# Keeping VectorE's unused allowance for one more unit, and computing the gates later, in a four-layer attention kernel

## Chip, cores and metric

The kernel runs on one core of a Trainium2 chip. A core has five engines that run side by side, each taking its own instructions strictly in order: TensorE (PE, matrix multiplication; PEld are its weight loads), VectorE (DVE), ScalarE (ACT, activation functions), GpSimd (POOL) and SyncE (SP, which issues the transfers here). Engines wait for each other through semaphores. The metric is the device time of one execution in microseconds (us); lower is better. The time before is 2142.66 us, the median of three runs (2138.74 to 2143.29).

## What is computed

Four layers over 2,048 tokens of width 512, with 32 heads of 16. Layers 0 and 2 (kind A) work in four segments of 512 tokens: causal attention inside a segment, mixed by a gate per head with a memory that earlier segments have filled. Layers 1 and 3 (kind B) are full attention over all tokens.

```python
def _A_ref(x, wq, wk, wv, wo, beta):           # N = 4 segments, per head
    ...
    g = _sigmoid(beta).reshape(1, H, 1, 1)
    for s in range(N):
        logits = jnp.einsum('bhqd,bhkd->bhqk', qs, ks) * scale + mask
        p = _softmax(logits, axis=-1)
        a_dot = jnp.einsum('bhqk,bhkd->bhqd', p, vs)
        pq = phi(qs)
        num = jnp.einsum('bhld,bhde->bhle', pq, M)
        den = jnp.einsum('bhld,bhd->bhl', pq, z)[..., None] + 1e-06
        outs.append(g * (num / den) + (1.0 - g) * a_dot)
        pk = phi(ks)
        M = M + jnp.einsum('bhld,bhle->bhde', pk, vs)
        z = z + jnp.einsum('bhld->bhd', pk)
    ...
def _B_ref(x, wqkv, wo):
    ...
    scores = jnp.einsum('bhqd,bhkd->bhqk', q, k) * Dh ** (-0.5)
    p = _softmax(scores, axis=-1)
    o = jnp.einsum('bhqk,bhkd->bhqd', p, v)
    ...
x = x + _A_ref(_layernorm(x), ...); x = x + _B_ref(_layernorm(x), ...)
x = x + _A_ref(_layernorm(x), ...); x = x + _B_ref(_layernorm(x), ...)
```

## The kernel before

The program is written out at build time by a planner (class `Builder`), which decides the order of every engine's instructions; the chip then follows that order.

**Units.** The attention work is cut into *units*. A unit takes up to three *banks*; a bank is 128 keys by 512 queries of scores for one head, made by TensorE from masked queries `qm` and keys (`KA`, `KB`). `unit` issues the score matmuls into one of two sets of three PSUM banks, and then one exponential by ScalarE over all three (line 1039, `pT<-ps`). Banks of kind A are also masked by GpSimd (line 1054). Two units later (three for kind A) `pv_step` multiplies the exponentials by the values (`VA`, `VB`), adding up in PSUM bank 6. Eight heads of a chunk and query segment are two *groups* of up to 64 banks each; when a group has all its products, `finish` has VectorE transpose the accumulator out of bank 6 (line 1099, `tT`), takes reciprocals of the softmax sums (line 1103), and GpSimd scales (line 1112). The next group accumulates into the same bank 6.

**VectorE's share of the exponentials.** `dx_pick` may take one more bank out of a group per unit and give its exponential to VectorE instead of ScalarE. Its scores go to PSUM bank 7; VectorE reads them out (`dx_first`, line 748), and once two such banks are there a chain of six instructions computes the exponential by a polynomial (`dx_chain`, lines 772 to 782, tiles `dxo`, `dxz`). `dx_pick` refuses while the VectorE allowance is below -300 ns, while a buffer or a spacing rule forbids it, or when little attention work is left in stock (`low`, under 24 banks).

**Background work.** Everything else (layer norms, projections, the memory, output projections, and the steps of `dx_chain`) is cut into steps held by generator tasks. A step says what it needs, how many halves of a PSUM bank's matmuls it costs on TensorE, and its nominal time on VectorE. Projections and outputs use PSUM bank 7 too. In each turn of the main loop `attention` issues one unit, then `credit` grants an allowance: 2 (kind A) or 3 (kind B) on TensorE and 1,300 or 1,420 ns on VectorE, or 5 and 2,600 when the stock is low. `background` then runs steps while both allowances are positive and VectorE's, with 300 ns of slack, covers the step. `finish` and the transposes of finished chunks (`run_deferred`) are charged to the same allowance. What a unit leaves unused does not carry over: `credit` caps the allowance at one unit's grant. An overdraft does carry over.

```python
858  def credit(self, pe, dve):
860      self.cr_pe = min(self.cr_pe + pe, pe)
861      self.cr_dve = min(self.cr_dve + dve, dve)
```

**Fillers.** `keep_busy` adds multiplications by a tile of zeros (`ps<-wB,zero`) so that TensorE has 1,024 columns of extra work in each unit.

**The gates.** `gates` computes sigmoid(beta) (`gtok`) and its complement per head (`omgT`): for each an exponential on ScalarE (line 427), an addition and a reciprocal on VectorE (lines 429, 430). They read two small tables, `bet` and `betT`, which five transfers on SyncE's queue fetch at the start. Before the change `task_A` calls `gates` for layer 0, segment 0, right after `ln_first` has issued the first layer norm and its transposes. `omgT` is used by `finish` of kind A (line 1106), `gtok` by the memory of later segments (line 606). The first key and query projections follow; their evictions (`evac`) alternate between VectorE (line 353, first keys) and ScalarE (line 351, first queries) while no unit has been issued.

Of the kernel before, what the change touches and what calls it, by code (L numbers as in the profile page):

```python
# [174 lines left out]
def bcast(ap, dims):  # L175
    return bass.AP(tensor=ap.tensor, offset=ap.offset, ap=[list(ap.ap[0])] + [list(d) for d in dims])
# [36 lines left out]
class Builder:  # L213
# [326 lines left out]
    def task_A(self, L, s):  # L540
        sl = s % 2
        need = [("x", L, s)]
        if s >= 2:
            need += [("attn", L, s - 2), ("mem", L, s - 2)]
        if s == 0 and L > 0:
            need += [("attn", L - 2, 2), ("attn", L - 2, 3), ("mem", L - 2, 2), ("mem", L - 2, 3)]
        yield need, 0, 0
        k = yield from self.ln_part(L, s)
        yield ["xT"], 0, 0
        slot = self.take_xT()  # L550
        if L == 0 and s == 0:
            yield from self.ln_first(k, slot)
            self.gates()
        else:
            yield from self.ln_tiles(L, s, k, slot)
            yield [("dma", ("xT", L, s))], 0, 0
        for c in range(NCH):
            yield from self.proj_fm(self.wA, self.b_wA[1], 512, slot, c, self.KA[:, sl, c, :], self.b_KA[sl][c])
            self.flags.add(("K", L, s, c))
            yield from self.proj_fm(self.wA, self.b_wA[0], 0, slot, c, self.QA[:, sl, c, :], self.b_QA[sl][c])  # L560
            self.flags.add(("Q", L, s, c))
            if c == 0:
                for ti in range(4):
                    yield from self.proj_tm(self.wA, self.b_wA[2], 1024, slot, ti,
                                            self.v_evac(self.VA[:, sl, ti, :], self.b_VA[sl][ti]))
                self.flags.add(("V", L, s))
        if s < 3:
            prev = (L, s - 1) if s else (L - 2, 3)
            read = [("dma", ("amemT",) + prev + (3,))] if prev[0] >= 0 and prev[1] else []
            yield ([("mem",) + prev] if prev[0] >= 0 else []), 0, 0  # L570
            old = [o for b in self.b_phk for o in b.reads.values()]
            for c in range(NCH):
                self.dma_tr(self.phk[:, :, c * 128:(c + 1) * 128], self.KA[:, sl, c, :], [self.b_KA[sl][c]], [self.b_phkc[c]],
                            ("phk", L, s), old)
            for j in range(2):
                yield [("dma", ("phk", L, s))] + read, 0, 0
                a, ba = self.phk[:, 2 * j:2 * j + 2, :], self.b_phk[2 * j:2 * j + 2]
                yield from self.phi(a, self.b_phkc + ba, a, ba)
            self.flags.add(("phk", L, s))
        self.give_xT(slot)  # L580
        if s > 0:
            for c in (0, 2):
                yield [("op", L, s - 1), ("mem", L, s - 1)] + ([("dma", ("amemT", L, s - 1, 3))] if s > 1 else []), 0, 0
                yield from self.phi(self.QA[:, sl, c:c + 2, :], self.b_QA[sl][c:c + 2], self.phq[:, c:c + 2, :], self.b_phq[c:c + 2])
            self.flags.add(("phq", L, s))
        self.flags.add(("proj", L, s))
# [271 lines left out]
    def credit(self, pe, dve):  # L858

        self.cr_pe = min(self.cr_pe + pe, pe)  # L860
        self.cr_dve = min(self.cr_dve + dve, dve)

    def background(self, bank=None):
        while self.cr_dve > 0 and self.cr_pe > 0:
# [216 lines left out]
    def finish(self, g):  # L1081

        bank = self.banks[6]
        acc = self.ps[:, bank.col0:bank.col0 + 512]
        if g.first and g.last:
            src, bsrc, bk, al = acc, [], bank, g.acc
        else:
            a, ba = self.accS(g)
            if g.first:
                self.op("dve", lambda e: e.tensor_copy(a, acc), writes=ba, bank=bank, alloc=g.acc)  # L1090
            else:
                self.op("dve", lambda e: e.tensor_tensor(a, a, acc, ALU.add), reads=ba, writes=ba, bank=bank, alloc=g.acc)
            if not g.last:
                return 700
            src, bsrc, bk, al = a, ba, None, None
        n = self.ring("tT", 1)
        tT = self.tT[:, n, :, :]
        bt = self.b_tT[n]
        self.op("dve", lambda e: e.transpose(tT.rearrange("p a b -> p (a b)"), src), reads=bsrc, writes=[bt], bank=bk, alloc=al)  # L1099
        m = self.ring("rd", 2)  # L1100
        rd = self.rd[:, m, :]
        br = self.b_rd[m]
        self.op("dve", lambda e: e.reciprocal(rd, tT[:, :, 16]), reads=[bt], writes=[br])  # L1103
        if g.kind == "A":
            om = self.omgT[:, g.c, g.e:g.e + 1]
            self.op("dve", lambda e: e.tensor_scalar(rd, rd, om, None, op0=ALU.mult), reads=[br, self.b_omgT], writes=[br])
        if g.e == 0:
            self.oi = self.ring("ob", 1)
        oi = self.oi
        rb = bcast(rd[:, 0:1], [[1, 16], [0, 16]])  # L1110
        ob = self.ob[:, oi, :, 16 * g.e:16 * g.e + 16]
        self.op("pool", lambda e: e.tensor_tensor(ob, tT[:, :, 0:16], rb, ALU.mult), reads=[bt, br], writes=[self.b_ob[oi][g.e]])  # L1112
        if g.e == 1:
            self.deferred.append((self.step + 2, g, oi))
        return 1100
# [54 lines left out]
    def attention(self):  # L1170
        self.flags = {("x", 0, s) for s in range(NSEG)}
        self.xT_free = [0, 1]
        self.dma_at, self.forcing = {}, False
        self.sel, self.pvq, self.deferred, self.qm_free = [], [], [], [0, 1, 2, 3]
        self.qm_late = []

        self.dx_free, self.dx_use, self.dx_bufs = list(range(self.NDX)), [0] * self.NDX, [0, 1]
        self.dx_build, self.dx_pairs, self.dx_now, self.dxq = [], [], [], []
        self.dx_step = self.misc_step = self.bank_step = -9
        self.bubble = True  # L1180
        self.forced, self.low, self.cur, self.gap = 0, True, None, 1
        self.nfin, self.oT_owner = {}, {}
        self.cr_pe = self.cr_dve = 0
        self.step = self.bg_cols = 0
        self.misc_banks = [7]
        self.make_groups()
        self.make_tasks()
        n = 0
        while True:
            items = self.take_banks()  # L1190
            if not items:
                if not self.seqA and not self.seqB and not self.pvq and not self.deferred and len(self.tasks) == 1:
                    break

                if self.pvq:
                    self.step += 1
                    self.pv_step(n + 9)
                    self.run_deferred(False)
                    continue
                self.misc_banks = [7, 0, 1, 2, 3, 4, 5]  # L1200
                self.bubble = True
                if not self.bg_one():
                    assert self.deferred, ("stuck", [t["next"] for t in self.tasks])
                    self.run_deferred(True)
                continue
            self.misc_banks = [7]
            if self.bubble:
                self.bubble, self.cr_pe, self.cr_dve = False, 0, 0
            self.step += 1
            self.near = self.ahead()  # L1210
            self.low = self.near < 24
            self.gap = 3 if self.near >= 400 else 1
            isA = items[0][0].kind == "A"
            split = not self.low and not isA
            self.unit(n, items, self.dx_pick(items))
            self.credit(5 if self.low else 2 if isA else 3, 2600 if self.low else 1300 if isA else 1420)
            if split:
                self.background(True)
            self.cr_dve -= self.pv_step(n)
            self.run_deferred(False)  # L1220
            self.background(False if split else None)
            if self.step > 10:
                self.keep_busy()
            self.bg_cols = 0
            n += 1
# [48 lines left out]
```

## Time and profile before

| | |
|---|---|
| median of the runs | 2142.66 us |
| the profiled execution | 2140.73 us, span 2138.6 us |
| mean granted TensorE clock | 0.966 |
| units in the plan | 1,495 |
| banks with their exponential on ScalarE / on VectorE | 4,484 / 380 |
| idle time of ScalarE before line 1039, put down to TensorE | 88.3 us |
| time TensorE waited for the transpose of line 1099 (matmuls; weight loads) | 29.8; 29.1 us |

The span is the time from the first to the last instruction that the profile shows. In groups, `out<-in` names tiles, then partitions x elements, the count, the busy time, the mean of one instruction in ns, and the idle time of the engine just before, with what ended it. In a timeline the columns are start, length, engine, line, operation, tiles, count, and in brackets the idle time before it with what ended it. An instruction's recorded length can overlap the one before on the same engine, so the time from one to the next is read from a stretch of many. The granted clock is the share of full speed that TensorE was allowed.

### The profile page before, as it was taken

The page shows a single profiled execution, that of the slowest core. Times are in us where ns is not written, and L with a number is a line of the kernel's source. Part 1 is how long each engine was busy: PE and PEld are TensorE (multiplying, and loading weights), DVE is VectorE, ACT ScalarE, POOL GpSimd, SP SyncE. Part 2 cuts the span into 40 slices and gives each one's busy share as a digit, 9 for nine tenths or more (in the row PEclk, how much of TensorE's full clock was granted, in tenths as well). Part 3 has the DMA queues.
Part 4 walks back from the last instruction along what each step waited for, and adds up shares of the span by engine and source line. Part 5 has one row for each costly group of instructions (what it writes and reads, how often), then busy time and mean ns, then how long its engine had stood idle before and what let it go on. Part 6 is the DMA issues. An engine that isn't in the chain of part 4 may idle for free.

```text
span 2138.6 us, 34960 instructions
## 1 busy us (share of the span) xinstructions
PE 1797.9 (84%) x13626; PEld 497.4 (23%) x13726; DVE 1591.0 (74%) x2806; ACT 2007.1 (94%) x1618; POOL 404.8 (19%) x833
## 2 busy tenths in 40 slices
PE   7788888878888988889888888888888888888887
PEld 3222222222222222222222222222222222222222
DVE  6665665487658885688857975548899999989996
ACT  5689998999989999899998999999999999999997
POOL 3532533020150002400033102401100000000000
PEclk9899999999999999899988999999999999999999
DMA  4011100000000000000000001000000000000000
GB/s 138 11 30 21 21 11 11 11 1 13 9 1 11 1 13 9 11 11 1 16 11 6 1 1 21 11 11 1 11 1 1 1 11 1 1 1 11 1 1 11
DMA packets 67142, 24.81 MB, mean 12 GB/s; under 512 B 59808, under 2 KB 66464, under 8 KB 66976
## 3 DMA queue, kind: packets, MB, share of 16 engines
q1 hardware_dynamic: 66976, 22.57, 4.7%
q8 instruction: 108, 1.77, 0.3%
q14 instruction: 58, 0.48, 0.1%
HBM read 6.30 MB, written 2.10 MB: 4 GB/s over the span
## 4 chain that ended last, share of the span: by engine, by line
issue 38%; ACT 26%; PE 14%; DVE 6%; POOL 4%; DMA 0%; SPq 0%; POOLq 0%; ACTq 0%; DVEq 0%
ACT pT L1039 25%; PE ps L337 14%; POOL ob L1112 2%; POOL pT L1054 1%; POOL qm L957 1%; DVE tT L1099 1%; DVE dxt L748 1%; DVE VB L353 1%; DVE dxo L782 0%; DVE KB L353 0%; DVE x L702 0%; DVE QB L353 0%; DVE VA L353 0%; ACT amem L528 0%; DMA xT<-xn 0%
## 5 line engine op out<-in xcount | busy, mean ns | idle before, releaser
L1039 ACT ACTIVATE pT<-ps 128x1536 bf16<-128x1536 f32 (+2 forms) x1589 | 1984.9, 1547 | 103.6 <-PE ps L337 88.3
L337 PE MATMUL ps<-qm,KB 32*128 32x512 bf16 x4096 | 509.9, 387 | 206.6 <-ACT pT L1039 188.9
L337 PE MATMUL ps<-wB,zero 128*17 128x512 bf16 x2092 | 642.8, 390 | 0.0
L337 PE MATMUL ps<-pT,VB 128*17 128x512 bf16 x3716 | 496.8, 386 | 20.7 <-DVE tT L1099 15.3
L748 DVE TENSOR_SCALAR dxt<-ps 128x512 uint32<-128x512 f32 x380 | 261.1, 687 | 93.4 <-PE ps L337 88.1
L1112 POOL TENSOR_TENSOR ob<-tT,rd 128x256 bf16<-128x256 f32 x128 | 100.1, 782 | 1198.7 <-DVE rd L1103 1158.2
L337 PEld LDWEIGHTS ps<-qm,KB 32*128 32x128 bf16 x4096 | 126.8, 91 | 750.5 <-ACT pT L1039 653.0
L1054 POOL TENSOR_SCALAR_AFFINE_SELECT pT<-pT 128x256 bf16<-128x256 bf16 (+2 forms) x512 | 208.4, 423 | 331.3 <-ACT pT L1039 321.9
L782 DVE SCALAR_TENSOR_TENSOR dxo<-dxt,dxz 128x1024 int16<-128x1024 uint16 (+1 forms) x203 | 235.2, 1159 | 4.6
L337 PEld LDWEIGHTS ps<-wB,zero 128*17 128x17 bf16 x2092 | 179.5, 92 | 115.1 <-issue 7.7
L337 PEld LDWEIGHTS ps<-pT,VB 128*17 128x17 bf16 x3716 | 115.5, 87 | 349.2 <-issue 298.4
L337 PE MATMUL ps<-dxo,VB 128*17 128x512 bf16 x380 | 146.6, 386 | 0.1
L776 DVE TENSOR_TENSOR dxz<-dxz,dxo 128x1024 f16<-128x1024 f16 (+1 forms) x203 | 134.8, 664 | 4.3
L337 PE MATMUL ps<-qm,KA 32*128 32x512 bf16 (+3 forms) x1024 | 109.3, 330 | 33.3 <-ACT pT L1039 25.3
L772 DVE TENSOR_SCALAR dxo<-dxt 128x1024 f16<-128x1024 uint16 (+1 forms) x203 | 133.6, 658 | 3.4 <-PE ps L337 3.2
L780 DVE TENSOR_TENSOR dxz<-dxz,dxo 128x1024 f16<-128x1024 f16 (+1 forms) x203 | 131.8, 649 | 2.1
L1099 DVE STREAM_TRANSPOSE tT<-ps 128x512 f32<-128x512 f32 x112 | 79.6, 711 | 72.1 <-PE ps L337 69.9
L337 PE MATMUL ps<-pT,VA 128*17 128x512 bf16 (+3 forms) x1024 | 106.0, 334 | 22.0 <-DVE tT L1099 14.2
L957 POOL TENSOR_SCALAR qm<-QB,par 128x512 bf16<-128x512 bf16 x102 | 81.1, 802 | 174.6 <-PE ps L337 174.6
L774 DVE TENSOR_SCALAR dxz<-dxo 128x1024 f16<-128x1024 f16 (+1 forms) x203 | 88.4, 435 | 6.8
L778 DVE TENSOR_SCALAR dxz<-dxz 128x1024 f16<-128x1024 f16 (+1 forms) x203 | 83.3, 410 | 6.7
L702 DVE TENSOR_TENSOR x<-x,ps 128x512 bf16<-128x512 bf16 x64 | 44.0, 687 | 54.8 <-PE ps L337 54.8
(92 smaller groups left out, 1019.3 us busy)
## 6 DMA issues: line engine op xcount, KB each, us to landing
out_dram<-x SPq DMA_DIRECT2D x8, 256.0 KB, 2.1
x<-in_A_x_dram SPq DMA_DIRECT2D x3, 512.0 KB, 11.8
wB<-in_B_wqkv_dram SPq DMA_DIRECT2D x1, 1536.0 KB, 13.6
xT<-xn SPq DMA_TRANSPOSE x60, 2.4
x<-in_A_x_dram SPq DMA_DIRECT2D x4, 128.0 KB, 2.2
wA<-in_A_wk_dram SPq DMA_DIRECT2D x1, 512.0 KB, 4.1
wA<-in_A_wq_dram SPq DMA_DIRECT2D x1, 512.0 KB, 5.5
wA<-in_A_wv_dram SPq DMA_DIRECT2D x1, 512.0 KB, 6.4
```

Source lines behind the costliest of these rows:

```text
L337: self.sc.add("pe", lambda e: e.matmul(out, lhsT, rhs, start=start, stop=stop, skip_group_check=True), reads=reads, banks=[(bank, "w", all ...
L748: self.op("dve", lambda e: e.tensor_scalar(self.dxt[:, b, i, :], o, SCALE * LOG2E * 65536, 127.0 * 65536, op0=ALU.mult, op1=ALU.add), writ ...
L772: self.op("dve", lambda e: e.tensor_scalar(f, lo, 2.0 ** -16, None, op0=ALU.mult), reads=bt, writes=bo)
L774: self.op("dve", lambda e: e.tensor_scalar(z, f, EXP_C3, EXP_C2, op0=ALU.mult, op1=ALU.add), reads=bo, writes=bz)
L776: self.op("dve", lambda e: e.tensor_tensor(z, z, f, ALU.mult), reads=bo + bz, writes=bz)
L780: self.op("dve", lambda e: e.tensor_tensor(z, z, f, ALU.mult), reads=bo + bz, writes=bz)
L782: self.op("dve", lambda e: e.scalar_tensor_tensor(ob, hi, 128.0, z, op0=ALU.mult, op1=ALU.add), reads=bt + bz, writes=bo)
L957: self.op(eng, (lambda m, q, col: lambda e: e.tensor_scalar(m, q, col, 0.0, op0=ALU.mult, op1=ALU.add))(m, q, col), reads=[bq, self.b_par] ...
L1039: self.sc.add("act", (lambda dst, src: lambda e: e.activation(dst, src, ACT.Exp, scale=SCALE))(dst, src), writes=self.b_pT[slot * 3 + i:sl ...
L1054: self.op("pool", (lambda blk, pat: lambda e: e.affine_select(blk, blk, pattern=pat, compare_op=ALU.is_ge, fill=0.0, base=0, channel_multi ...
L1099: self.op("dve", lambda e: e.transpose(tT.rearrange("p a b -> p (a b)"), src), reads=bsrc, writes=[bt], bank=bk, alloc=al)
L1112: self.op("pool", lambda e: e.tensor_tensor(ob, tT[:, :, 0:16], rb, ALU.mult), reads=[bt, br], writes=[self.b_ob[oi][g.e]])
```

## The change

`credit` now caps VectorE's allowance at one unit's grant plus 1,200 ns, so that up to 1,200 ns left by one unit can be spent in the next. TensorE's allowance is capped as before. The planner then makes another plan: 424 banks go to VectorE instead of 380, and 1,480 units are issued instead of 1,495.

`gates` is no longer called from `task_A`; `attention` calls it in the second turn of the main loop (`step` 2), after that unit's background steps. An assertion at build time in `finish` states that `omgT` has been written before it is used.

```diff
@@ task_A
             yield from self.ln_first(k, slot)
-            self.gates()
         else:
@@ credit
         self.cr_pe = min(self.cr_pe + pe, pe)
-        self.cr_dve = min(self.cr_dve + dve, dve)
+        self.cr_dve = min(self.cr_dve + dve, dve + 1200)
@@ finish
         if g.kind == "A":
+            assert self.b_omgT.last_write is not None and self.step > 2
             om = self.omgT[:, g.c, g.e:g.e + 1]
@@ attention
             self.background(False if split else None)
+            if self.step == 2:
+                self.gates()
             if self.step > 10:
```

## The prediction

> **What bounds the kernel now.** I read the page's busy shares first, then the groups by form, then windows over the long stretches of the schedule, and last the timeline where ScalarE stands idle.
>
> ```profile
> PE 1797.9 (84%) x13626; PEld 497.4 (23%) x13726; DVE 1591.0 (74%) x2806; ACT 2007.1 (94%) x1618; POOL 404.8 (19%) x833
> ```
>
> ScalarE is busy 94% of the span and VectorE 74%; the change moves work from the first to the second. But shares are means over stages. The windows below (columns: stretch, length, then busy us and instructions of PE, weight loads, VectorE, ScalarE, GpSimd; granted clock; DMA) are the last pass of layer 1 and the three 149-unit passes of layer 3.
>
> ```profile
> 1146.70:1250.50 103.80, 87.98 (x680) 22.93 (x677) 95.30 (x149) 102.34 (x77) 11.31 (x12) 0.98 0.00 1
> 1523.20:1725.80 202.60, 169.73 (x1316) 43.50 (x1314) 187.24 (x289) 200.67 (x150) 14.82 (x16) 0.98 0.01 4
> 1725.80:1927.70 201.90, 170.46 (x1315) 43.89 (x1313) 181.43 (x283) 200.83 (x151) 14.78 (x16) 0.98 0.01 4
> 1927.70:2127.90 200.20, 166.41 (x1303) 43.04 (x1304) 179.02 (x278) 200.20 (x150) 12.64 (x14) 1.00 0.01 4
> ```
>
> ScalarE sets the pace there: the last pass is 149 units in 200.20 us, ScalarE never idle, so 1.3436 us is the floor of a unit (one exponential over three banks). VectorE is busy 92% in the first of the three. So the same kernel has one engine full and a second nearly full for its last quarter.
>
> Where ScalarE does lose time in these passes, it is at the end of a group of scores. One case, from the timeline and from windows over it:
>
> ```profile
> 1576.88 0.70 DVE L1099 STREAM_TRANSPOSE tT<-ps 128x512 f32<-128x512 f32 x1
> 1577.63 0.61 PE L337 MATMUL ps<-pT,VB 128*17 128x512 bf16 x4 [0.74 <-DVE tT L1099]
> 1579.74 1.45 ACT L1039 ACTIVATE pT<-ps 128x1536 bf16<-128x1536 f32 x1 [0.60 <-PE ps L337]
> ```
>
> ```profile
> 1576.50:1577.60 1.10, 0.39 (x3) 0.09 (x3) 1.08 (x2) 1.10 (x2) 0.00 (x0) 0.93 0.00 0
> 1577.60:1579.00 1.40, 1.36 (x6) 0.25 (x6) 0.88 (x3) 1.40 (x2) 1.05 (x2) 0.50 0.00 0
> 1579.00:1581.00 2.00, 2.00 (x12) 0.42 (x11) 1.73 (x2) 1.40 (x2) 2.00 (x2) 0.53 0.04 8
> ```
>
> VectorE came late to the transpose that empties the accumulator bank (L1099); TensorE, which takes its work in order, stood idle for most of a microsecond, and then its granted clock was 0.50 for 3.4 us. The next scores came late and ScalarE lost 0.60 and then 0.25 us. Over the last three passes this happened at four of 24 group ends, for 0.5 to 1.2 us each (0.95 in the mean).
>
> The start is a wait of another kind:
>
> ```profile
> 9.49 1.02 ACT L489 ACTIVATE xT<-ps 128x1024 bf16<-128x1024 bf16 x1 [7.41 <-PE ps L341]
> 16.04 0.21 ACT L427 ACTIVATE omgT<-betT 128x8 f32<-128x8 bf16 x1 [5.09 <-DMA betT<-in_A_beta_dram]
> 16.15 0.58 ACT L351 ACTIVATE QA<-ps 128x512 bf16<-128x512 f32 x1
> ```
>
> ScalarE waits 5.09 us for the last of four small transfers, and the eviction of the first queries is queued behind that wait; the first scores start at 17.56.
>
> **The gates, moved.** Two activations and four VectorE instructions (0.23, 0.21, then 0.18, 0.35, 0.17, 0.20 us) go behind the second unit; none is added and no transfer moves. In the built order the query eviction now follows the transposed-x copy directly. The first eight projection matmuls end at 12.86, so eviction (0.58) ends near 13.5, and the first scores start as long after it as now (17.56 against 16.73, so 0.83 later): 14.2. That is 3.3 us saved. At the new place the data landed at 16.0, before the second exponential ends (22.0 now, 18.7 then), so nothing waits. If that cover failed, the wait would stand in front of the third exponential and give up to 3 us back; the upper bound is the 5.1 us wait itself. I take -3.3, with 0 and -5.1 as ends. The first second-segment x tiles land at 17.5, and VectorE would reach them at about 17.3, so 0.2 us of waiting hides nothing.
>
> **The allowance.** Each unit gives background work on VectorE a nominal 1,300 (layer kind A) or 1,420 ns (kind B); what is left over was dropped, now up to 1,200 ns stay. The plan that comes out has 1,480 units instead of 1,495: 424 banks of scores, not 380, take VectorE's exponential. Row by row:
>
> ```profile
> L748 DVE TENSOR_SCALAR dxt<-ps 128x512 uint32<-128x512 f32 x380 | 261.1, 687 | 93.4 <-PE ps L337 88.1 <-DVE dxo L782 0.3
> L782 DVE SCALAR_TENSOR_TENSOR dxo<-dxt,dxz 128x1024 int16<-128x1024 uint16 x177 | 217.2, 1227 | 3.9
> L776 DVE TENSOR_TENSOR dxz<-dxz,dxo 128x1024 f16<-128x1024 f16 x177 | 123.5, 698 | 3.7
> L772 DVE TENSOR_SCALAR dxo<-dxt 128x1024 f16<-128x1024 uint16 x177 | 122.1, 690 | 3.4 <-PE ps L337 3.2
> L780 DVE TENSOR_TENSOR dxz<-dxz,dxo 128x1024 f16<-128x1024 f16 x177 | 120.5, 681 | 1.6
> L774 DVE TENSOR_SCALAR dxz<-dxo 128x1024 f16<-128x1024 f16 x177 | 79.6, 450 | 6.0
> L778 DVE TENSOR_SCALAR dxz<-dxz 128x1024 f16<-128x1024 f16 x177 | 75.6, 427 | 5.8
> ```
>
> 44 first steps at 687 ns are 30.2 us; 20 more pairs at 690+450+698+427+681+1,227 = 4,173 ns are 83.5; four more single banks at 2,635 ns (the 512-wide rows of the same lines) are 10.5; two fewer accumulations are -1.4. VectorE gets 122.8 us more work, 1,714 in all. TensorE's work is the same but for 24 fewer fillers of zeros.
>
> *What it saves.* 15 units at 1.3436 us: -20.1 us, if ScalarE stays the bound (the lower end is 0, where VectorE is). Besides, the old plan ran short of scores near 1,400 us (11 units in its "low" state, and a pair of groups split for lack of keys); the 11 units from 1411.1 to 1430.4 took 19.3 us against 14.8 at the floor. The new plan has no such stretch: -4, between 0 and -4.5.
>
> *What it costs.* Kept allowance is spent in one go: background runs of three or four chain steps in a unit, 2.9 us of VectorE work, where the old plan's units in layer 1 stayed under 2.3. I summed the planned VectorE work ahead of each group end at the rows' durations, against 1.3436 us a unit. The largest excess over the units ahead was 0.5 us in the mean for the three long passes of layer 1 and 0.8 for those of layer 3; it becomes 1.6 and 2.0. Behind the late transpose TensorE's next accumulation is queued, behind that the next scores, behind these ScalarE. Sorted by lateness, eight transposes of the trace of before that start 0.66 us (mean) after the last accumulating matmul cost ScalarE 0.13 us each, the eight next at 0.78 us 0.35, and a dropped clock costs 0.95. These 48 group ends lose 8 us now (measured). Lower end: no more than now. Upper end: three in four at 1.2 us, 43 in all. A lost microsecond on ScalarE is also one in which VectorE catches up, so I take half of them at 1.1: 26, that is +18.
>
> [...]
>
> In the first 64 units VectorE gets 5 us more work while ScalarE already waits about 0.5 us a unit: +2, between -4 and +6.
>
> **Sum.** -3.3 - 20.1 - 4 + 18 + 2 = -7.4 us on the profiled execution, which took 2140.73 (span 2138.6): 2133.3. The runs' median is 2142.66, 1.9 higher; I say 2134.
>
> **Rivals.** *Paid in full.* Group ends lose no more than now: -3.3 - 20.1 - 4 = -27.4, 2113. For it: TensorE is idle 16% and absorbs delay. Against: the four losses above happened with less excess. [...]
>
> *VectorE becomes the bound in layer 3.* Its three passes get 10 more banks (27.7 us) on 547.7 busy, plus some 25 ns between instructions for 887 of them: 597 us, against 595 for ScalarE's 443 units. If VectorE also keeps 20 of the 31 us in which it now waits there for TensorE, they take 617, 13 more than now, and the four units saved there (5.4) are not a gain: -3.3 - 14.7 - 4 + 2 + 13 + 9 (layer 1's group ends) = +2: 2143.
>
> [...]
>
> **How the numbers follow.** Below 0.2% (4.3 us) this kernel's measurement can't tell a change from none. Forecast (2124 to 2142): 0.40; of it faster 0.33, same 0.07. Paid in full: 0.13, faster. VectorE bound: 0.15; same 0.12, slower 0.03. Dropped clock: 0.32; slower 0.31, same 0.01. So faster 0.46, same 0.20, slower 0.34. The range reaches from near "paid in full" to past the dropped clock, 2116 to 2154; the forecast's own is 2124 to 2142.
>
> **What would show it.** First scores near 14.2 us (gates). ScalarE's 1,536-wide group at 1,352 instructions and its busy time some 25 us lower (units). No idle ScalarE between units near 1,400 us (starved stretch). The wait of TensorE on the L1099 transpose (58.9 us before, matmuls and weight loads together) about doubled, and the granted clock in the long passes below 0.98 (group ends). It would be wrong if these waits stay as they are, or if VectorE shows over 97% in layer 3 with ScalarE idle all along rather than at group ends.

## The result, and the profile after

The changed kernel took 2204.68 us (median of six runs, 2202.8 to 2209.21) against 2140.7 us for the kernel before in the same session (2135.58 to 2143.76). The ratio is 1.0305, with a 95% interval of 1.0287 to 1.0324: it is slower by 3%, above the predicted range of 2116 to 2154. The profiled execution took 2209.21 us with a span of 2207.0 us, 68.4 us more than before's 2138.6; its mean granted clock is 0.955 (0.966 before). In the changed kernel the lines behind `task_A` have moved up by one: L1038, L1098, L747, L781 are L1039, L1099, L748, L782 of before.

The page's busy times of the changed kernel, and its group of exponentials over three full banks (columns: count, busy us, mean ns of one, idle us before them and what ended it), with the same group of before under it:

```profile
PE 1824.2 (83%) x13599; PEld 499.8 (23%) x13702; DVE 1697.2 (77%) x2992; ACT 1999.9 (91%) x1597; POOL 403.4 (18%) x833
```

```profile
L1038 ACT ACTIVATE pT<-ps 128x1536 bf16<-128x1536 f32 x1352 | 1850.9, 1590 | 141.8 <-PE ps L337 125.4 <-POOL ob L1112 4.7 <-POOL Mz L644 3.7
```

```profile
L1039 ACT ACTIVATE pT<-ps 128x1536 bf16<-128x1536 f32 x1366 | 1857.8, 1686 | 81.1 <-PE ps L337 71.0 <-POOL pT L1054 4.1 <-POOL ob L1112 2.5
```

The work moved as planned: 1,352 such exponentials (1,366 before) and 106 us more on VectorE. But ScalarE now idles 125.4 us in this group because of TensorE (71.0 before), and its recorded busy time fell by only 7.2 us. The kernel traded work for waiting.

Where the time went is read stage by stage (start of a stage to start of the next, from the windows):

| stage | before, us | after, us | difference |
|---|---|---|---|
| start to the first long pass of layer 1 | 471.7 | 477.5 | +5.8 |
| long passes of layer 1, layer 2 in between | 778.8 | 838.9 | +60.1 |
| first pass of layer 3 (with the starved stretch) | 272.7 | 270.0 | -2.7 |
| last three passes of layer 3 | 604.7 | 611.0 | +6.3 |
| rest | 10.7 | 9.6 | -1.1 |

Nearly all of the loss is in the second row. In the windows (columns as in the prediction's), first of the changed kernel: that stretch, one part pass of layer 1 in it, and the last three passes of layer 3:

```profile
477.50:1316.40 838.90, 694.36 (x5093) 190.71 (x5134) 626.27 (x1079) 747.70 (x604) 141.79 (x300) 0.94 0.04 7
642.10:765.00 122.90, 102.00 (x698) 27.23 (x700) 95.69 (x158) 105.69 (x77) 6.51 (x12) 0.94 0.03 5
1586.40:1792.10 205.70, 171.10 (x1317) 43.73 (x1315) 193.75 (x307) 200.42 (x149) 15.01 (x16) 0.98 0.01 4
1792.10:1995.00 202.90, 171.04 (x1312) 43.98 (x1314) 192.78 (x302) 199.68 (x149) 14.04 (x16) 0.98 0.01 4
1995.00:2197.40 202.40, 170.73 (x1296) 43.13 (x1293) 178.62 (x282) 198.91 (x148) 13.52 (x14) 0.98 0.01 4
```

The same stretch and the same part pass of the kernel before:

```profile
471.70:1250.50 778.80, 666.66 (x5107) 186.43 (x5145) 582.07 (x1019) 747.59 (x603) 143.46 (x298) 0.96 0.04 8
623.90:729.00 105.10, 92.83 (x704) 25.73 (x707) 88.44 (x150) 104.80 (x78) 7.79 (x14) 0.99 0.04 6
```

ScalarE has the same 747.6 us of work in both, so what was added is idle time. VectorE isn't full there either: 626 of 839 us, 75%, so this is no stage that has run out of VectorE.

The view of waits in that stretch names the engine that waited, the tile and line it waited with, and whom for; then us in total, number of times, longest. The changed kernel:

```profile
ACT pT L1038 <- PE ps L337: 85.6, 87, 6.1
...
PEld ps L337 <- DVE dxt L747: 38.8, 56, 1.9
...
PE ps L337 <- DVE dxt L747: 26.4, 31, 1.8
...
PEld ps L337 <- DVE tT L1098: 22.3, 19, 2.7
PE ps L337 <- DVE tT L1098: 21.4, 23, 2.4
...
PEld ps L337 <- DVE x L701: 10.2, 13, 2.3
```

The kernel before:

```profile
ACT pT L1039 <- PE ps L337: 25.4, 30, 3.6
...
PEld ps L337 <- DVE tT L1099: 12.2, 19, 1.1
PE ps L337 <- DVE tT L1099: 10.4, 20, 0.9
...
PEld ps L337 <- DVE dxt L748: 5.3, 19, 0.6
...
PE ps L337 <- DVE dxt L748: 1.2, 3, 0.5
```

ScalarE's wait for TensorE rose by 60.2 us, the stage's whole loss. TensorE in turn waits for VectorE. The wait on the transposes out of bank 6, which the prediction priced, doubled (matmuls: 10.4 to 21.4). The wait on `dxt`, the read of bank 7, was almost nothing and became the largest of TensorE's waits on VectorE (matmuls: 1.2 to 26.4).

One such wait in the timeline of the changed kernel, from the part pass above:

```profile
748.97 1.04 PE L337 MATMUL ps<-xT,wB 128*128 128x512 bf16 x4
749.57 0.43 DVE L777 TENSOR_SCALAR dxz<-dxz 128x1024 f16<-128x1024 f16 x1
...
750.03 0.69 DVE L779 TENSOR_TENSOR dxz<-dxz,dxo 128x1024 f16<-128x1024 f16 x1
...
750.76 1.22 DVE L781 SCALAR_TENSOR_TENSOR dxo<-dxt,dxz 128x1024 int16<-128x1024 uint16 x1
751.90 0.68 DVE L353 CAST QB<-ps 128x512 bf16<-128x512 f32 x1
...
752.64 0.39 PE L337 MATMUL ps<-qm,KB 32*128 32x512 bf16 x1 [1.99 <-DVE QB L353]
...
754.21 10.90 ACT L1038 ACTIVATE pT<-ps 128x1536 bf16<-128x1536 f32 x8 [2.00 <-PE ps L337]
```

A projection into bank 7 is complete at 750.01. VectorE still has two chain steps in front of the eviction (lines 779 and 781) and reads the bank only at 751.90. TensorE does the products and scores that stand next in its order, to 750.65 (rows left out above); then comes the score matmul of an extra bank, into the same bank 7. It neither reads `QB` nor feeds ScalarE's next exponential, but TensorE takes its work in order, so the products and scores behind it wait 1.99 us, and ScalarE 2.00.

### The profile page after: what moved, and what is told of

It is laid out like the page before. It is cut to its first block, busy times and chain, and to the rows that moved or that the text cites. A ratio compares the mean times of both kernels' runs of the same rounds, so it can differ in the third digit from the quotient of the medians.

```text
span 2207.0 us, 35009 instructions
## 1 busy us (share of the span) xinstructions
PE 1824.2 (83%) x13599; PEld 499.8 (23%) x13702; DVE 1697.2 (77%) x2992; ACT 1999.9 (91%) x1597; POOL 403.4 (18%) x833
## 4 chain that ended last, share of the span: by engine, by line
issue 35%; DVE 26%; PE 21%; ACT 12%; POOL 4%; DMA 1%; SPq 0%; POOLq 0%; ACTq 0%; DVEq 0%
PE ps L337 21%; ACT pT L1038 12%; DVE dxt L747 3%; DVE dxo L781 3%; DVE dxz L775 2%; DVE dxo L771 2%; DVE dxz L779 2%; POOL ob L1112 2%; POOL pT L1053 2%; DVE tT L1098 1%; DVE dxz L773 1%; DVE dxz L777 1%; POOL qm L956 1%; DVE lnst L444 1%; DVE x L701 1%
## 5 line engine op out<-in xcount | busy, mean ns | idle before, releaser
L1038 ACT ACTIVATE pT<-ps 128x1536 bf16<-128x1536 f32 (+3 forms) x1568 | 1976.3, 1468 | 173.7 <-PE ps L337 156.6
L337 PE MATMUL ps<-qm,KB 32*128 32x512 bf16 x4096 | 538.4, 393 | 197.6 <-ACT pT L1038 151.1
L747 DVE TENSOR_SCALAR dxt<-ps 128x512 uint32<-128x512 f32 x424 | 290.4, 685 | 91.0 <-PE ps L337 88.5
L781 DVE SCALAR_TENSOR_TENSOR dxo<-dxt,dxz 128x1024 int16<-128x1024 uint16 (+1 forms) x227 | 263.6, 1161 | 4.2
L337 PE MATMUL ps<-dxo,VB 128*17 128x512 bf16 x424 | 164.6, 392 | 0.4 <-DVE dxo L781 0.4
L775 DVE TENSOR_TENSOR dxz<-dxz,dxo 128x1024 f16<-128x1024 f16 (+1 forms) x227 | 150.8, 664 | 5.8
L771 DVE TENSOR_SCALAR dxo<-dxt 128x1024 f16<-128x1024 uint16 (+1 forms) x227 | 150.4, 662 | 5.5 <-PE ps L337 3.6
L779 DVE TENSOR_TENSOR dxz<-dxz,dxo 128x1024 f16<-128x1024 f16 (+1 forms) x227 | 150.8, 664 | 5.0
L1098 DVE STREAM_TRANSPOSE tT<-ps 128x512 f32<-128x512 f32 x112 | 79.5, 710 | 64.6 <-PE ps L337 64.6
L956 POOL TENSOR_SCALAR qm<-QB,par 128x512 bf16<-128x512 bf16 x102 | 85.3, 845 | 186.5 <-PE ps L337 182.9
L773 DVE TENSOR_SCALAR dxz<-dxo 128x1024 f16<-128x1024 f16 (+1 forms) x227 | 96.2, 424 | 6.0
L777 DVE TENSOR_SCALAR dxz<-dxz 128x1024 f16<-128x1024 f16 (+1 forms) x227 | 94.8, 417 | 6.1
L337 PE MATMUL ps<-xT,wA 128*128 128x512 bf16 x227 | 68.4, 404 | 23.2 <-DVE dxt L747 9.0
## 6 DMA issues: line engine op xcount, KB each, us to landing
wB<-in_B_wqkv_dram SPq DMA_DIRECT2D x1, 1536.0 KB, 12.3
x<-in_A_x_dram SPq DMA_DIRECT2D x4, 128.0 KB, 2.2
```

Of the source, the lines that this page charges most:

```text
L337: self.sc.add("pe", lambda e: e.matmul(out, lhsT, rhs, start=start, stop=stop, skip_group_check=True), reads=reads, banks=[(bank, "w", all ...
L747: self.op("dve", lambda e: e.tensor_scalar(self.dxt[:, b, i, :], o, SCALE * LOG2E * 65536, 127.0 * 65536, op0=ALU.mult, op1=ALU.add), writ ...
L771: self.op("dve", lambda e: e.tensor_scalar(f, lo, 2.0 ** -16, None, op0=ALU.mult), reads=bt, writes=bo)
L773: self.op("dve", lambda e: e.tensor_scalar(z, f, EXP_C3, EXP_C2, op0=ALU.mult, op1=ALU.add), reads=bo, writes=bz)
L775: self.op("dve", lambda e: e.tensor_tensor(z, z, f, ALU.mult), reads=bo + bz, writes=bz)
L777: self.op("dve", lambda e: e.tensor_scalar(z, z, EXP_C1, None, op0=ALU.add), reads=bz, writes=bz)
```

## Experiments

Every run below was compared with the kernel before in the same session (whose median lay between 2140.7 and 2146.4 us from session to session). Three quantities per run, from its profiled execution:

- *Over floor*: the span less 1.3436 us for every unit issued, the floor taken from the last pass of before.
- *Bank 6*: idle time of TensorE's matmuls (gaps over 0.15 us) that ended with VectorE's read of the accumulator.
- *Bank 7, other*: the same, ended by any other VectorE work but the masked queries. In before 22.3 of its 33.2 us are reads of bank 7 (`dxt`, projections, outputs), in the changed kernel 85.3 of 99.9.

The expectations count some of the reads that move a group's partial sums out of bank 6 with bank 7; so they have 102 and 55 us for the changed kernel where the table has 99.9 and 57.2.

| run | what | units / VectorE banks | ratio (95%) | span | bank 7, other | bank 6 | over floor |
|---|---|---|---|---|---|---|---|
| before | | 1,495 / 380 | 1 | 2138.6 | 33.2 | 34.5 | 130.0 |
| after | the change | 1,480 / 424 | 1.0305 (1.0287-1.0324) | 2207.0 | 99.9 | 57.2 | 218.4 |
| e1 | gates alone | 1,495 / 380 | 0.998 (0.9961-0.9999) | 2134.7 | 36.6 | 37.8 | 126.0 |
| e2 | allowance alone | 1,480 / 424 | 1.031 (1.0273-1.0347) | 2203.0 | 97.6 | 59.9 | 214.4 |
| e3 | none kept, grant 1,500 | 1,489 / 398 | 0.9943 (0.9922-0.9964) | 2128.7 | 39.4 | 35.1 | 128.0 |
| e4 | unit's work under 1,720 ns | 1,495 / 379 | 0.9985 (0.9971-0.9999) | 2142.1 | 40.7 | 32.4 | 133.4 |
| e5 | quiet unit after a burst | 1,483 / 415 | 1.0584 (1.0544-1.0624) | 2268.0 | 111.4 | 74.1 | 275.5 |
| e6 | kept except in the last passes | 1,485 / 410 | 1.0245 (1.02-1.029) | 2197.1 | 82.1 | 55.6 | 201.8 |
| e7 | kept in the last passes only | 1,494 / 382 | 1.0047 (1.0025-1.007) | 2154.1 | 42.6 | 39.6 | 146.7 |
| e8 | 150 ns kept | 1,489 / 398 | 0.9942 (0.9916-0.9968) | 2129.4 | 37.8 | 33.7 | 128.8 |
| e9 | extra banks not in bank 7 | 1,480 / 424 | 1.0033 (1.0015-1.0052) | 2150.2 | 43.2 | 59.0 | 161.7 |
| e10 | final transposes not from bank 6 | 1,480 / 424 | 1.0165 (1.0125-1.0204) | 2174.2 | 105.6 | 12.0 | 185.7 |
| e11 | both | 1,480 / 424 | 0.9875 (0.9835-0.9915) | 2111.2 | 53.1 | 11.8 | 122.6 |
| e12 | both, on before | 1,495 / 380 | 0.9819 (0.9777-0.9861) | 2098.9 | 28.8 | 4.2 | 90.2 |
| e13 | e11, evictions not from bank 7 | 1,480 / 424 | 0.9695 (0.9679-0.9712) | 2077.1 | 27.0 | 8.1 | 88.6 |
| e14 | the same, on before | 1,495 / 380 | 0.971 (0.9694-0.9727) | 2076.0 | 12.6 | 2.5 | 67.3 |
| e15 | work under 1,850 ns | 1,487 / 405 | 1.008 (1.0063-1.0097) | 2154.3 | 51.1 | 52.9 | 156.3 |
| e16 | 150 kept, kind A grant 1,500 | 1,489 / 399 | 1.0052 (1.0032-1.0072) | 2149.1 | 64.9 | 40.5 | 148.5 |
| e17 | 150 kept, grant 1,460, under 1,940 | 1,489 / 397 | 1.0007 (0.9995-1.0019) | 2136.6 | 34.1 | 38.8 | 136.0 |
| e18 | 300 kept, grant 1,460, under 1,850 | 1,490 / 396 | 0.9967 (0.9952-0.9981) | 2133.9 | 44.8 | 33.5 | 131.9 |

### Which half of the change: e1, e2

```diff
@@ e1: credit
-        self.cr_dve = min(self.cr_dve + dve, dve + 1200)
+        self.cr_dve = min(self.cr_dve + dve, dve)
@@ e2: task_A, attention
+            self.gates()
...
-            if self.step == 2:
-                self.gates()
```

> The gates behind the second unit, the allowance capped as before; 1,495 units and 380 banks on VectorE, as before. All theories: first scores 2.6 us earlier (15.6 against 18.2 us for the first exponential in the changed kernel's trace), so about 2.6 us (0.1%) faster than before, within the measurement. If the move itself cost time later, it would be slower than before.

> The kept allowance alone, gates where they were. All of the 64 us loss should be here: 2205 to 2210 us, ratio about 1.03. If the two parts work on each other, clearly less.

The gates alone made the kernel 4.0 us shorter by the span (the interval of the ratio, 0.9961 to 0.9999, only just excludes no change); the allowance alone carries the whole loss. In e1's timeline the first exponential starts at 14.37 (18.2 before), and the gates' first activation follows it without a wait:

```profile
14.37 2.79 ACT L1038 ACTIVATE pT<-ps 128x1536 bf16<-128x1536 f32 x2 [0.88 <-PE ps L337]
17.05 0.23 ACT L427 ACTIVATE gtok<-bet 128x32 f32<-128x32 bf16 x1
```

### More work or work in bursts: e3, e4

Two theories were left: VectorE has too much work (424 banks), or it has it in one go. e3 gives it more work evenly; e4 keeps the allowance but limits what one unit spends.

```diff
@@ e3: credit, attention
-        self.cr_dve = min(self.cr_dve + dve, dve + 1200)
+        self.cr_dve = min(self.cr_dve + dve, dve)
...
-            self.credit(5 if self.low else 2 if isA else 3, 2600 if self.low else 1300 if isA else 1420)
+            self.credit(5 if self.low else 2 if isA else 3, 2600 if self.low else 1300 if isA else 1500)
@@ e4: the choice of a background step, attention
-        if pick is None or (slack is not None and pick["next"][2] > 0 and self.cr_dve + slack < pick["next"][2]):
+        if pick is None or (slack is not None and pick["next"][2] > 0 and (self.cr_dve + slack < pick["next"][2] or self.cr_top - self.cr_dve + pick["next"][2] > 1720)):
...
+            self.cr_top = self.cr_dve
...
+            spent = self.cr_top - self.cr_dve
...
+            self.cr_top = self.cr_dve + spent
```

> Gates moved; nothing kept, but a grant of 1,500 instead of 1,420 ns for units of kind B: 398 banks on VectorE (18 of the change's 44 more), 1,489 units, and hardly a unit with over 2,400 ns of planned VectorE work more than before (7 against 4; the changed kernel has 170). Theory 'load' (more VectorE work makes the time): 18/44 of the loss of 64 us, 2160 to 2170. Theories of bursts (work of several steps in one unit comes late, and TensorE waits behind it, at bank 7 or at group ends): 6 units fewer, so 2130 to 2140.

> The changed kernel, but a unit's background may not bring its VectorE work over 1,720 ns: the allowance is kept and yet the plan has 1,495 units and 379 banks on VectorE as before; units over 2,400 ns are 2, units over 2,000 ns 145 (before 29, changed 250). Theory 'load': as before, about 2138. Theory of bursts: between before and the changed kernel by how many bursts are left; if those over 2,400 ns alone hurt, 2140 to 2145; if those over 2,000 too, 2160 to 2180.

e3 put 18 more banks on VectorE than before and issues six units fewer (8.1 us); its span is 6.0 us below that of e1, which has the same gates. More work by itself costs little at that size. e4 shows the other side less well, since its plan ended at 379 banks: without bursts of over 2,400 ns the loss is gone, but so is the extra work. It came out in the range given for the case that only those over 2,400 ns hurt, though its plan has 145 units over 2,000 ns, where before has 29.

### Keeping bursts away from bank 7: e5

`dx_pick`, and the choice of a background step that uses TensorE, got one more reason to refuse, `self.step - self.burst_step < 2`, and `attention` sets it:

```diff
+            if top - self.cr_dve > 2000:
+                self.burst_step = self.step
```

> The changed kernel with one rule more: in the unit after one with over 2,000 ns of planned VectorE work, no new work starts in PSUM bank 7 (no extra bank of scores, no projection or output). The bursts stay (127 units over 2,400 ns, 249 over 2,000; changed 170 and 250), as do most of the savings (1,483 units, 415 banks). Theory 'bank 7' (TensorE waits for bank 7, which late VectorE has not read out): most of the loss gone, 2130 to 2155. Theory 'group ends' (TensorE waits for the late transpose of bank 6): the transposes are as late as in the changed kernel, 2185 to 2210.

This made it worse, a span of 2268.0, far from what either theory had said. It isn't the clean test that it was meant to be, since the rule also moves the other users of bank 7; perhaps it presses them closer together between the bursts, which was not measured. In e5's waits of the whole run:

```profile
PEld ps L337 <- DVE QB L353: 30.0, 29, 2.7
...
PEld ps L337 <- DVE VA L353: 28.8, 26, 5.2
PEld ps L337 <- DVE dxt L747: 25.7, 42, 1.9
```

In the changed kernel these three are 18.3, 18.6 and 45.0 us: the wait on `dxt` fell, and the waits on evictions of projections from the same bank rose by more, together with those of bank 6.

### Where the allowance does harm, and how much of it: e6, e7, e8

```diff
-        self.cr_dve = min(self.cr_dve + dve, dve + 1200)
@@ e6
+        self.cr_dve = min(self.cr_dve + dve, dve + (0 if self.sel and self.sel[0].L == 3 and self.sel[0].qseg else 1200))
@@ e7
+        self.cr_dve = min(self.cr_dve + dve, dve + (1200 if self.sel and self.sel[0].L == 3 and self.sel[0].qseg else 0))
@@ e8
+        self.cr_dve = min(self.cr_dve + dve, dve + 150)
```

> Allowance kept everywhere but in the three long passes of layer 3 (1,485 units, 410 banks). Theory 'bank 7': the loss sits where projections and outputs share bank 7 with the extra scores, so nearly all of it: 2185 to 2200. Theory 'group ends': about half, as 24 of 48 long-pass group ends keep the old plan, and those with the larger excess: 2165 to 2180.

> The counterpart: allowance kept only in the three long passes of layer 3 (1,494 units, 382 banks; 124 units over 2,000 ns). 'Bank 7': little other work in bank 7 there, 2138 to 2146. 'Group ends': 24 group ends late, 2160 to 2175.

> 150 ns kept instead of 1,200: 1,489 units and 398 banks, the same two counts as with the grant of 1,500 (2132 us), but 54 units over 2,400 ns of planned VectorE work instead of 7, and 98 over 2,000 instead of 33. If the burst and not the sum of work makes the time, slower than 2132 by about 54/170 of the loss: 2145 to 2160. If not, 2130 to 2136.

Over the floor e6 lies 71.8 us above before and e7 16.7, together 88.5; the change lies 88.4 above it. So the two parts of the program add up, and about four fifths of the harm is done outside the last passes. That they agree to 0.1 us is luck: the profiled execution of e7 took 2156.43 us against a median of 2150.6, and the gates' 4 us are in all three. e7 lies between what the two theories had said. With 150 ns kept instead of 1,200 (e8) the plan still has 54 units over 2,400 ns, and the harm expected of them did not come. VectorE takes 18 more banks than before and loses next to nothing by waiting: ScalarE's wait on TensorE is near that of before (88.3), and so is that of TensorE's weight loads on late transposes (29.1).

```profile
ACT pT L1038 <- PE ps L337: 93.2, 150, 4.7
...
PEld ps L337 <- DVE tT L1098: 31.5, 46, 1.7
```

### The two banks taken away: e9 to e14

These kernels keep the plan and the number of VectorE's instructions, but take away what makes TensorE wait; the work that is left out with it is missing from their output. They also spare VectorE some of its own waits for TensorE's matmuls (410 us in the changed kernel, 336 in e9, 269 in e11, 170 in e13, summed over gaps above 0.15 us), so that it can run ahead; they don't separate what of the gain comes from that. In e9 `dx_first` reads a tile of `x` in place of bank 7 (709 ns in the mean, 685 in the changed kernel), and a filler of zeros stands for the score matmul; in e10 `finish` transposes a tile of `x` in place of the accumulator, for groups that are not summed over several passes; e11 has both. In e13 the evictions on VectorE (line 353) read a tile of `x` as well. e12 and e14 are e11 and e13 on the kernel before.

```diff
@@ e9: dx_first, unit
-        o = self.ps[:, bank.col0:bank.col0 + 512]
+        xf = self.x[:, 0:2, :].rearrange("p a b -> p (a b)").bitcast(dt.float32)
...
-            bank7, al7 = self.misc(), self.new_alloc()
...
+            bank7, al7 = None, None
+            self.bg_cols -= 512
@@ e10: finish
-            src, bsrc, bk, al = acc, [], bank, g.acc
+            src, bsrc, bk, al = self.x[:, 0:2, :].rearrange("p a b -> p (a b)").bitcast(dt.float32), self.b_x[0:2], None, None
@@ e13: evac
-            self.op("dve", lambda e: e.tensor_copy(dst, src), writes=bdst, bank=bank, alloc=al)
+            self.op("dve", lambda e: e.scalar_tensor_tensor(dst, xf, 1.0, zf, op0=ALU.mult, op1=ALU.add),
+                    reads=[self.b_fz] + self.b_x[0:2], writes=bdst)
```

> The changed kernel, its plan and its VectorE instructions the same, but the extra banks of scores no longer go through PSUM bank 7: their score matmul is left out (one more filler of zeros stands for it), and VectorE's first step (as long, with two operands in SBUF) reads x instead of bank 7. 'Bank 7': the wait of TensorE for bank 7 (102 us of idling in the changed kernel, 33 before) falls to 30 or less, time 2130 to 2155. 'Group ends': 2185 to 2205. 'The plan itself is worse, whoever waits': 2195 to 2210.

> The changed kernel with bank 7 as it was, but the transpose at a group's end reads x instead of the accumulator (for groups that are not summed over several passes), so the next group need not wait for it; as many instructions on VectorE. The heads' results are left out of the output. 'Bank 7': TensorE's idling for bank 6 goes (55 us to about 10), that for bank 7 stays; 2165 to 2195. 'Group ends': 2130 to 2150.

> Both edits on the changed kernel. If the two waits on late VectorE are all of the loss, the plan's saving shows: below the kernel before, 2095 to 2125. If the plan costs otherwise (more units short of work, VectorE as the bound), 2140 or more.

> Both edits on the kernel before, as a control: what the same waits cost there. Its plan has 15 units more than the changed one (20 us) and a stretch short of scores (4 us): if both kernels are then bound by ScalarE, it is 15 to 30 us slower than the run before this one, 2115 to 2145. If it is as fast or faster, the changed plan is the worse one even without waits.

> The changed kernel with both edits of the run that took away bank 6 and the extra banks in bank 7, and one more: VectorE's evictions of the projections read x instead of bank 7 (as long, one instruction with two SBUF operands each). TensorE then waits for no late eviction of a projection. If these are the rest of the loss: 2080 to 2095, and no slower than the kernel before with the same edits. If not: 2105 to 2115.

> The same three edits on the kernel before: 2085 to 2100 (its bank 7 waits were 29 us of TensorE's idling after the first two edits, 56 in the changed kernel). If the evictions are the rest, the changed kernel is up to 20 us faster than this one; if the rest is VectorE's load in the last passes or the order of the work, it stays slower.

e9 is 56.8 us shorter than the changed kernel, and TensorE's idle time in the column of bank 7 is 56.7 us smaller. Its waits of the whole run (line 339 is line 337 of the others):

```profile
ACT pT L1038 <- PE ps L339: 107.1, 149, 4.4
...
PE ps L339 <- DVE tT L1098: 48.4, 54, 2.8
```

ScalarE's wait fell from 156.6 to 107.1, while TensorE's wait on the transposes of bank 6 stayed (45.2 in the changed kernel). e10 takes most of these away: 32.8 us shorter, with 45.2 us less idle time at bank 6 and 5.7 more in the other column. Both together, e11, are 95.8 us shorter.

That is not yet the change's loss, because the same removal makes before shorter too, by 39.7 (e12), which had been expected 15 to 30 us slower than e11 and is faster. What the change costs over before shrinks from 68.4 us to 12.3 (e11 against e12) with both edits, and to 1.1 when VectorE's evictions of projections no longer hold bank 7 either (e13 against e14; by the medians of three runs each, 2076.17 and 2079.68, e13 is even 3.5 us shorter). So all but a few us of the loss goes when VectorE's reads of the two banks no longer hold TensorE up. Even in e13 the 15 units saved are worth 20.2 us and nearly all of that is given back: 19.9 us more TensorE idle time behind VectorE is left, among it waits for the outputs and for operands that VectorE makes.

Is it simply VectorE that is full at the end? e11's window over the second of the last three passes, 148 units, says no:

```profile
1703.20:1902.00 198.80, 180.10 (x1315) 48.83 (x1312) 193.58 (x300) 198.80 (x150) 18.71 (x16) 1.00 0.01 4
```

VectorE is busy 97% of it, ScalarE is never idle, and a unit takes 198.80 / 148 = 1.343 us: the floor.

### Can one have more banks without the waits: e15 to e18

e15 is e4 with 1850 in place of 1720. The others change what is kept and the grant; e17 and e18 also have e4's bound, at 1940 and 1850.

```diff
@@ e16 (e17: 150 and 1300 if isA else 1460; e18: 300 and 1300 if isA else 1460)
-        self.cr_dve = min(self.cr_dve + dve, dve + 1200)
+        self.cr_dve = min(self.cr_dve + dve, dve + 150)
...
-            self.credit(5 if self.low else 2 if isA else 3, 2600 if self.low else 1300 if isA else 1420)
+            self.credit(5 if self.low else 2 if isA else 3, 2600 if self.low else 1500 if isA else 1420)
```

> The changed kernel (1,200 ns kept, gates moved), with a unit's background bounded so that its planned VectorE work stays under 1,850 ns: 1,487 units, 405 banks on VectorE, 57 units over 2,000 ns (changed 250, before 29) and 41 over 2,400 (170, 4). Bursts make the time: 2125 to 2135, faster than before by the 8 units and the gates. The kept allowance makes it, however it is spent: 2160 to 2190.

> Gates moved, 150 ns kept, and a grant of 1,500 instead of 1,300 ns for units of kind A: 1,489 units, 399 banks, 92 units over 2,000 ns and 46 over 2,400, 23 units short of scores instead of 40. As the run with 150 ns kept: 2125 to 2135; if the earlier layer work of kind A matters, up to 5 us less than that run.

> Gates moved, 150 ns kept, a grant of 1,460 ns, a unit's background bounded to 1,940 ns: 1,489 units and 397 banks on VectorE, as the runs with 150 ns kept or a grant of 1,500 have. Planned VectorE work ahead of its reads of banks 6 and 7 (what is over 0.9 us, summed over all reads) is 44 us, against 48 in the kernel before, 87 and 88 in those two runs and 112 in the one with the 1,850 ns bound. If lateness at these reads makes the time: TensorE idles 65 us or less for banks 6 and 7 together and the time is 2115 to 2128. If the count of units and bursts alone, 2128 to 2134; if the kept allowance, 2140 or more.

> 300 ns kept, a grant of 1,460, a bound of 1,850 ns: 1,490 units, 396 banks, planned lateness 51 us by the same sum. Lateness: 2118 to 2130. The kept allowance (twice that of the run before): slower than that run by 5 us or more.

All four were chosen by what their plans show (units whose VectorE work runs over 2 us, and a sum of planned lateness at banks 6 and 7), and all four came out slower than that said: by 23, 16, 14 and 5 us over the upper ends given. e17's plan was to leave 65 us of TensorE idle time at most in both columns; 72.9 was measured. e15 and e16 are slower than before, e17 is no different from it, e18 a little faster. None reaches e3 and e8, which stay the best: 0.9943 and 0.9942, some 12 us below before, of which the gates are 4. Both are faster than either kernel of the change.

### All runs together

Over the 20 profiled kernels the time over the floor follows TensorE's idle time behind VectorE (both columns together): the correlation is 0.987, with a slope of 1.1 us per us and 49 us where that idle time is none. From before to after the idle time rises by 66.7 (bank 7, other) + 22.7 (bank 6) = 89.4 us, the time over the floor by 88.4. Less 15 units, 20.2 us, that leaves the 68 us of the span. A correlation alone could have a common cause; e9 to e11, where the waits were taken away and the plan left as it was, are what shows the direction. Nor is the slope the price of a single wait.

## Why the prediction was wrong

**The step that failed** is the one headed "What it costs". It began rightly, with the kept allowance spent in one go, in runs of three or four chain steps (by the plans 170 units hold over 2,400 ns of VectorE work, 4 before). It then priced one victim of a late VectorE, the transposes out of bank 6 at the 48 group ends, and no other. Bank 7 has no term in the sum, though the text on the kernel says that extra banks, projections and outputs share it. TensorE's idle time behind VectorE's reads of bank 7 rose from 22.3 to 85.3 us, by 63.0, which at 1.1 us of span for each (all runs together, above) makes some 70. On the profiled execution 2133.3 was forecast and 2209.21 measured, 75.9 more: the miss has about the size of this term. The trace of before didn't advertise it: of its 22.3 us only 1.2 were waits of matmuls on `dxt` (6.0 on the weight loads), the rest on projections and outputs. A wait that is small because its cover is just sufficient is not a wait that can't grow; the right question was what cover it had. VectorE's own waits for the matmuls that `dx_first` reads stayed as they were (88.1 us before, the page's L748 row, 88.5 after), so many of its reads are as prompt as ever. But those late enough to hold up a matmul rose from 3 to 37 over the run.

**Group ends, +18.** The mechanism was there and the size near: TensorE's idle time at bank 6 rose by 22.7 us. Its wait on the transpose, matmuls and weight loads together, went from 58.9 to 89.5 us, by half rather than to about double. In the last three passes 6.3 us were lost although four fewer units (5.4 us) were issued there: 11.7. (The 0.95 us that it took for one dropped clock is between two ways of counting the four cases in before: ScalarE's idle time in the timeline is 0.73 us in the mean, 0.26 to 1.00, and the time over the floor in the three passes 1.0.)

**Fewer units, -20.1.** The 1,480 units came as planned, but no run shows the gain by itself. With most waits removed (e13 against e14) it was still eaten by the 19.9 us of idle time that was left. ScalarE's busy time fell by 7.2 us where 25 had been said, though the count of exponentials is right. An exponential that stands alone is recorded with 1.45 us, one in a row costs 1.34, and ScalarE has 81 more waits on TensorE in the run (211 against 130): about 9 us by that. The rest is open. In e13 against e14, where few waits are left, its busy time is 18.0 us lower (1979.4 and 1997.4). VectorE has the 186 more instructions that were summed, but 106 us more busy time instead of 122.8.

**Starved stretch, -4.** Not shown. The first pass of layer 3 is 2.7 us shorter, but ScalarE is idle in it for as long as before: 270.00 less 255.69 busy is 14.3 us, and 272.70 less 258.45 was 14.3. From 1,418 to 1,484 us it has single gaps of some 0.2 to 0.9 us again and one of 1.2, so the sign that the prediction named, no idle ScalarE there, did not come.

**Gates, -3.3.** Right. In e1 the first exponential comes 3.8 us earlier and the span is 4.0 shorter. In the profiled execution of the changed kernel it comes 2.6 us earlier, since there the first queries' eviction waited 3.65 us for TensorE instead of 2.39. Its projections ran at a granted clock of 0.50 from 12 to 14 us; in the kernel before it was 1.00 in that stretch:

```profile
14.17 0.60 ACT L351 ACTIVATE QA<-ps 128x512 bf16<-128x512 f32 x1 [3.65 <-PE ps L337]
15.65 2.79 ACT L1038 ACTIVATE pT<-ps 128x1536 bf16<-128x1536 f32 x2 [0.88 <-PE ps L337]
18.33 0.23 ACT L427 ACTIVATE gtok<-bet 128x32 f32<-128x32 bf16 x1
```

No bracket stands before the gates: at the new place nothing waits, as was said.

**Early units, +2.** Not measured apart. In e2, with the gates where they were, the 13th transpose of line 1099 starts 0.5 us later than in before (114.49 against 114.03), which speaks for a small term. But the sum stopped there: the whole start up to layer 1's long passes lost 5.8 us in spite of the gates' 2.6, so 8.4.

**The rivals.** Slower came out, and its chance of 0.34 lay nearly all on a dropped clock (0.31). The chain was the one of "What it costs" (late read, TensorE in order, ScalarE starved), the place another: the dips to 0.50 in the last three passes of before sit at group ends, most of the loss was at bank 7, and in the case of the timeline TensorE waited 1.99 us for bank 7 and the clock stayed at 1.00. Nor did every late transpose of before have a dip behind it: TensorE idled 0.74 us behind the one that starts at 1576.88, and the clock fell to 0.50; 0.93 us behind the one at 1602.31, and it stayed at 1.00 (windows from 1602.3 to 1608.7). "VectorE becomes the bound in layer 3" did not happen: the changed kernel loses 6.3 us there with VectorE at most 95% busy, and that pass of e11 holds the floor with VectorE at 97%. "Paid in full" leaned on TensorE's idle 16%. In the case of the timeline that idle time absorbed nothing: 1.99 us of waiting in the middle of TensorE's queue came out as 2.00 us on ScalarE.

Taking work off the busiest engine, here ScalarE (94%), paid only up to a point: 18 banks taken off it with a small carry (e8) gave -12 us, 44 with the large one +64, the same gates in both. While units are issued, everything but their scores and their products goes through bank 7 alone, and more than half of TensorE's idle time behind VectorE is there (85.3 of 157.1 us). A second such bank was not tried, since the kernel's eight (two sets of three for scores, 6 and 7) are all in use.

**What stays open.** Two things. First, which property of a plan foretells the wait: neither the count of bursts nor the sum of planned lateness did (e8 came out 15 us below the range given for bursts, e15 to e18 5 to 23 us above theirs). Second, how the loss divides between waiting and the lower granted clock. In the stretch of layers 1 and 2 the same matmuls took 694.4 us instead of 666.7, at a granted clock of 0.94 instead of 0.96; no run separates that from the waits.

## What to carry to other kernels

Before giving an engine more work in larger portions, list every buffer that it empties for an engine that takes its work in order, and ask of each how long its read may be late before the next write waits. A wait that is near zero in the profile may be one that has just enough cover: TensorE's on `dxt` in layers 1 and 2 went from 1.2 to 26.4 us. Allowances that carry over turn an even load into bursts; here a slightly larger even grant (e3) or a small carry (e8) gave 18 more banks and, with the gates, 0.6%, where 1,200 ns gave 44 and cost 3%.

## What the runs showed of the hardware

- VectorE ran at 97% of a 200 us pass (e11: 193.58 of 198.80 us) without ScalarE losing time, in a kernel where most of TensorE's waits on it were taken away. In the changed kernel, at 94% (193.75 of 205.70), ScalarE lost time.
- The mean granted clock was lower, by and large, in the kernels whose TensorE idled more behind VectorE: 0.955 in the changed kernel (157.1 us of it in both columns), 0.966 before (67.7), 0.981 in e12 (33.0); over the 20 profiled kernels the correlation is -0.92. It was 1.00 in the pass of e11 shown. What sets it for a single wait was not shown: after the 1.99 us of idle TensorE in the timeline, up to 752.64, the clock stayed at 1.00 in the windows of 1.6 and 2 us behind it.
